# Residual buffer rows of 258 values and a newly searched instruction order in a Performer-attention and Fourier-mixing kernel

## The chip, the cores and the metric

The kernel runs on one core of a Trainium2 chip. The core has five engines with instruction queues of their own: TensorE (PE in the profile, with its weight loads listed apart as PEld), VectorE (DVE), ScalarE (ACT), GpSimd (POOL) and SyncE (SP), which here issues nearly all of the DMA transfers. Each engine takes its instructions strictly in the order in which they stand in the program; between engines, semaphores hold an instruction back until what it needs is there. The metric is the device time of one execution in microseconds (us), lower is better. Everything is computed in fp32.

## What is computed

The reference has two blocks. The first is attention with random positive features for 8 batches of 8 heads, 576 positions and head size 64; the second is a Fourier mixing with a two-layer network behind it.

```python
def phi(x):                                   # 128 features per position
    h = einsum('bhsd,md->bhsm', x, omega) - sum(x * x, -1, keepdims=True) / 2
    return exp(h - max(h, -1, keepdims=True)) / sqrt(m)
q_p, k_p = phi(q * scale), phi(k * scale)
kv, z = einsum('bhsm,bhsd->bhmd', k_p, v), sum(k_p, axis=2)
attn = einsum('bhsm,bhmd->bhsd', q_p, kv) / (einsum('bhsm,bhm->bhs', q_p, z)[..., None] + 1e-6)
x = attn.transpose(0, 2, 1, 3).reshape(8, 576, 512)
u = x + real(fft(fft(x, axis=1), axis=2))
un = (u - mean(u, -1)) / sqrt(var(u, -1) + 1e-6)
out = u + maximum(un @ w_ch1, 0) @ w_ch2      # 512 -> 2048 -> 512
```

The two weight matrices come as 64-bit floats and are turned into fp32 on the chip.

## The kernel before

The work has two parts. **The first part** holds all of the attention, all of the mixing, the conversion of the weights, and the network for the first 512 rows ("plain" blocks, four of 128 rows). **The second part** does the network for the other 4096 rows in eight blocks of 512, by a scheme of seven products in place of eight on halves (`first_of` for the first layer, L1359; `product_of` for the second, L1539).

Attention goes by pairs of heads, 32 pairs, up to three at a time (`attn`). A pair loads its keys and queries (L398, L401) and its values (L406), turns them on TensorE in two groups (`transposed`, L525), evicts these from PSUM on ACT or DVE (L564, L566), multiplies with omega (L644), takes the negative row maximum on DVE (L587) and the exponential on ACT (L604), forms the key-value product (L678, kept by L692 or L694), turns the query features (L525 again), and forms numerator and denominator (L725, L733). DVE then divides (L742, L743, L754) into the tile `x` of the batch.

When the four pairs of a batch are there, `mix` runs its Fourier mixing. Rows are added and subtracted in mirrored pairs ("folds": L782, L784, L788, L798, L811, with small copies at L818, L820 and L823), then TensorE multiplies with cosine and sine tables along the sequence (L844, L854, and L915 for a middle column), the result is evicted (L867) and multiplied along the model size (L894). `residual` brings these products together: ACT copies one half into the first plane of the tile `bmp` (L943), DVE forms difference and sum in the planes `mi` and `pl` (L948, L951), and `summed` adds these to `x` in two instructions, one of them reading backwards (L960, L961). The rows go out to DRAM (L975, L930, L986).

A block of the weights comes as raw 64-bit words (L492) and takes two steps on ACT or POOL (L461; L467 or L469), two on DVE (L472, L474) and one on POOL (L478). When all are converted, `w2_parts` forms the sums of the second weight matrix that the second part needs (L1240, 44 instructions of one size on DVE or POOL) and writes them to DRAM. The plain blocks are normalised (L1072 to L1078), turned (L525, evicted at L1091), multiplied with the first matrix (L1143, rectified at L1127 on DVE or L1129 on ACT) and the second (L1166), and added to their rows (L1179).

What sets the order is not the sequence of the code. Each of these streams is a Python generator that yields a `Step` ahead of its instructions: the engine or a choice of engines, an estimated length, what it waits for, which buffers and PSUM banks it takes and gives back. `Listing.run` picks one waiting step after another and so lays down one order for all engines. For the first part the picks are written out in the string `PICKS`, two characters a step: which of the waiting streams is next, and which engine and bank it gets. There the estimated lengths do not choose anything. For the second part there are no picks, and the planner chooses by estimated times.

A step marked `port=True` is one that the planner does not let run on DVE and POOL at the same time. TensorE runs matmuls in several shapes of its array, which the planner calls modes: the whole array, halves, quarters, and row tiles.

Of the kernel before, what the change touches and what calls it, by code (L numbers as in the profile page):

```python
# [31 lines left out]
NL = 2  # L32
# [7 lines left out]
class Clock(NamedTuple):  # L40
# [25 lines left out]
    "0808d258d8f8c3f8d408d8d6c8c8c8c4e8c8e8d0f8g8f6f858f8g8c8a8b848d2dhd0e2dhd8e8e8b0dhc6d8d488f8ghg8j8c8c890l2k8l6"  # L66
    "i8jhi8j2m8ihlhe888a0l6m4m892j8jhbhl8l818i8i0k888g6k8e2k8i8j878bhd8g8e6i8i4j8i8f8j2j8f8i0k6f8a8b8e8k8i8d2jhehf0"
    "e878i8e8f8i8h8g8g8f4f8g8g8b2d0e8g8b8g898e8h8ghchb6j8b2jhi0j8d6j8h4jhb88hj8j8g0d8e2m8i6m8h8l0m898n8j4h8o8o8g8n8"
    "d2m8m8m8k8k4l8l828l8f8l8a8e2e8f6k8b8f8j8k8e808e878h0j8j4j8d6jhh8j8i0ihehi8ihg4l0l8m8f8g2f6k8k878j0j85878e8h8f8"
    "h8d8h8h888g8b2g8b6g888a078f858i8e8i8f878a2787884h858h878d8d2f8f8g8g8ghc8e4h8i8i8jhb8hhb0j8j6j8j088l8c8j8a8gh78"  # L70
    "88h6h8f852k4k888l8i8j8e0khk6k8k0m2j8j8m8b8i898h8k8a4k8k8j87hh8bhc6j4c8k888g8k8c8d8e872i8f878j888l8b6n858c8n8e8"
    "70m8l8j6o0nhn8n4nhb8j6n2d8lhm0l8l8d8c8gh88k8g4k8k8i8f89868d6h8h888d89868g0g8b8g4h2h8f2h8d8h8hhhhe8f0i8i6j8j468"
    "68g8k8g8g8c2h8h8h088i8g8d6i8i8e8c488i8a878a890hhe8h8d808f8f89868g6h0g858j858l8d8g864j8l8gh88a8k8g8a8b852h8d4i8"
    "70jhi8j8g8c8f6j8k8i8j868c8a8a8j888i870e894i8i2i886ihi4i8f258j868j8b6k8f8j8g8i848a8i8i8d4h8b6i8i8h8i898c8h832ih"
    "e8i2ihi0ih7hi878h8e8i8b6l48hk84hi8j8k898k852k8g0n4nh56k8o8o8k8l883k0o88658p8d8n0p4o8q8k2j898j8o8o8688hn8n8n8kh"
    "k0i8l1n2o6nhj8k8o8n8d2n8n8e878hhgh78k8k84hl8g8j8k8f7e8b458j8j8h8g8e8g8i8h8l8l878b8k2l0k8k88896khc8g8i2i8i0ihg4"
    "i888e8l8c8chd6m8c8b0m8c8l2mhb6m8n8l0m8m6k8h8l8dhehb8n8n8h8g2n8h8o8g4n858e8e8i6l8h8i0l6lhk858k8g882kh98c8j8j868"
    "i86898h8g8a8g84870f8f896g4g8b2h4hhghe868h8j8d6l8l848488898j0jh7854i872i8f8i8i8i8h3k8g6e878k0d4j8g2j8k898i0l2l8"
    "a878dhj8f4l5l8d6l8jhd2k8b5ahj8c8j8i858i8jhg6i8g888j8h8k8e4j8j8c8j8j8b8i882i86878h8h8g4g8a6g8h8a870f8d4h2g8i8i8"
    "ih6838e8j8j8j8d8k83888i896d8j4k868g8m8ahm8f882mhm0m8d4m8m2l0n8lhk8986868h4l2e860b8d8b8e8o8f8n8e8m8m8l8l8l846l8"  # L80
    "h888l84892l8d8l8h8k8l868b878m884m8g8m8l2pho898f8n8fhe0n8n8m8i8c8d8d8b8e8d8j8g8f8n2d0oho4o8g8k8d8k088h8h858b4ih"
    "i2k8j898k8i0k8c8l8l8d4a8e8l898l8983898k8d898dhc88808f8f86880d8g8g868g8e2fhd84864e8d8e8d8d832dha88892d894d8c0dh"
    "c2e4e8d8d2e8f890a8f7g2b8ch88che85878d8d890dhb8b89876b874c0b89hdhd8d8d8c8d882c8c838ch66d7chch7h72c4d0dh78d8d8d8"
    "78d6dh989862b8b8a4c0b8c4b8c6b8e8c89848d8d862dha8d8c3d4e5f2d8che4f6e8e8e7f3e8a8f8f8f8bhd5f488g85898b8a8d8d8d8a8"
    "b8c8d6088898b864ch8hc8chchb0c6d2c8bh2834c8c89896b8bh3852b8b0b898b4b8b6b89268c8c8chc880d4d858883888d8d8dha8d8d8"
    "dhb8483638e758g8g844h8h2i4h840l8l8i8l88858k8k858j8j87h98i8i8b8i88858h862g8b8g8f4f8i67h68j8a87818i8f8e8e8i8a8h8"
    "h8h868g8g8ghc8g8b2h8c8c8c8g8g8g8g878f852h4hhh0h8g8h8e8h838f8c8g878c0g8g4g8f8g8g8e2f8bhehb8e6f4e858d848e868e842"
    "e6f0d8g838c8g8c8547hd8d872fha848e826f4f8c0h2i3f8689hi8i8a8c8g8g8188888c8a89874e0d8b8e898f882g5a8ehg8g8hhb872g8"
    "h8g6chghc0a8i8g1fhhha8h8h8f836h8h858g8a8a08hg4fh42f8ghg4gh78f0d8e8b8f8c698a2fhhhh8h8h8a864e0d892ihd8a8h8e875ah"
    "hhf8c6h2d8h0g8k8i8j8f838i8c4ih48i8h5iha2i8i8ahd8h874g8h8h8h8g8e6g8c828f2h8c8h4hhd8g0gha2g8g4h6i0h8387hi878d888"  # L90
    "g8b278f4h6g8a8h8d8g8g8b8d8e8e890e1f8d808f8i8b2ihh8d8i868i6j4b8h828g8f8h8h4d208ghf8c8c6h2g82858h8e80834g8d8d8e8"
    "a8f888a4b8f6g2e8ehehf8f896b8d8b8b2e4d8b8e6e8ch82d4b6c838d858d8b8d8b818a8d828787278c6c8c4c8b8c808c8c85868c8c864"
    "c848a8a6e298d8ch64d8e8d2e8f8d848d8d87hd8188660e8c8d8d8783862c8d894d8e87h50chd6c868d8d8b838c4ch087870a876b8b2b8"
    "d8a8a8e8e894fhf6f8ah84g6fhche8a8b0f8f438eh62f84868d878c840b8a888b86498a298c8a880bh46b8d864d8d888d870c8c4c8283h"
    "c8687878b0b8b238c846b8b47868808884887h8882b688c8c888c854b8b0b888b894c0c8bhb46858b8b87058a8489h9842484898468818"
    "388848407h4828487268707h68446h4842582h6h70886h787836783478704638a858782286489898688888684476686h2h3058425h5458"
    "265858324858585h246830687878568884224088b868649838183828786692a3589848981h9898686784957h933808282h28284276845h"
    "08988848785h80744h585898a8a82858368091a79ha108325h0h28283h38356408787808181268787878887h7848566878580h58285h4h"
    "3268387818587828688828682818483838381828280h180808"
# [203 lines left out]
def kernel(  # L303
# [149 lines left out]
    def narrow(i, dst, raw):  # L453
# [16 lines left out]
        yield Step(DVE, 0.34, take=("sign",), port=True, bias=0.19)  # L470
# [61 lines left out]
    def transposed(src, name, groups, after, makes, give, order=None):  # L532
# [3 lines left out]
        for j0, j1 in groups:  # L536
            m = j1 - j0
            yield Step(
                PE,
                0.03 + 0.056 * m,  # L540
                mode="rows",
                after=after(j0, j1),
                take=("duo",) + (("turned",) if j0 == 0 else ()),
                give=give(j0, j1), bias=0.14,
            )
# [65 lines left out]
    def attn(n):  # L611
# [18 lines left out]
        def pairs_of(js, *ts):  # L630
# [3 lines left out]
                (0.24 if wide else 0.22) * len(js),  # L634
# [26 lines left out]
        def feature(c):  # L661
# [6 lines left out]
            1.06,  # L668
# [18 lines left out]
        def keep():  # L687
# [23 lines left out]
            1.17,  # L711
# [26 lines left out]
        yield Step(DVE, 0.335, after=(("frame", b),), bias=-0.07)  # L738
# [27 lines left out]
    def mix(b):  # L766
# [8 lines left out]
        def folds(n):  # L775
# [18 lines left out]
            step = Step({DVE: 0.85, POOL: 1.6}, port=True)  # L794
            yield step
            eng = nc.gpsimd if step.eng == POOL else nc.vector
            for dst, o in ((NC3, ALU.add), (1, ALU.subtract)):
# [7 lines left out]
                {DVE: 1.13, POOL: 2.1},  # L805
# [24 lines left out]
        for n, (tab, name) in enumerate(((cs, "cs"), (sn, "sn"))):  # L830
            yield Step(
                PE,
                1.9,
# [42 lines left out]
        for c in range(NC3):  # L876
# [3 lines left out]
                0.97 if c < NL else 0.55,  # L880
# [25 lines left out]
    def middles(b, mid_t, mid_k):  # L906
        yield Step(PE, 0.5, mode="halves", after=(("fold", b, 0), "cs"), take=("bank",))
# [19 lines left out]
    def mirrored(b, x):  # L927
        yield Step(SP, 1.15, 2.6, after=(("sum", b, 1), ("sum", b, 2)), makes=("uh", b), kb=512, bias=-0.92)
# [6 lines left out]
    def residual(b, c, x, abb, mid_k):  # L935
# [4 lines left out]
        bmp = fft.tile([P, 3, KD], F32, name="bmp", tag="bmp", bufs=2)  # L940
        bs, mi, pl = (bmp[0:np_, n, :] for n in range(3))
# [13 lines left out]
        def summed(g, left, right):  # L955
            step = Step({DVE: 0.68, POOL: 1.3}, port=True)
# [102 lines left out]
    def norm_of(j, t, i, pool, dst, block=None, after=()):  # L1059
# [11 lines left out]
        yield Step(DVE, 1.12 if pool is mlpp else 1.01, after=after, bias=4.0 if after else -0.23)  # L1071
# [10 lines left out]
        yield Step(PE, 0.25, mode="rows", take=("duo",), give=("u",))  # L1082
# [598 lines left out]
```

## Time and profile before

| | |
|---|---|
| median of 3 runs | 1186.29 us (1183.14 to 1188.23) |
| profiled execution, its own time | 1184.3 us |
| its span, first to last instruction | 1182.5 us |
| granted TensorE clock, mean | 0.996 |
| busy in the span: PE, PEld | 1140.8 us, 1016.3 us |
| busy in the span: DVE, ACT, POOL | 767.1 us, 435.1 us, 412.4 us |
| HBM read, written | 179.24 MB, 43.25 MB |

The profile is of one execution. The kernel's lines carry the numbers that the text uses (L960 is line 960). In groups of instructions, "x16" is the number of instructions, then comes their busy time in us, the mean of one in ns, and behind the bar how long the engine had stood idle just before them and what ended that wait. A matmul of fp32 stands in the trace as two records. "Busy" for TensorE counts from the start of a matmul to its modelled end, and neighbours overlap, so the pace is read from start to start. An idle time with the releaser "issue" is one in which the engine waited for nothing that the profile shows.

### The profile page before, as it was taken

The numbers are of one execution on the slowest core, as the hardware profiler recorded it, in microseconds if no ns is written. First come the engines' busy times: TensorE is split into PE (matmuls) and PEld (weight loads), VectorE is DVE, ScalarE is ACT, GpSimd is POOL, SyncE is SP. The second block draws the span as 40 slices with busy tenths as digits, with TensorE's granted clock in tenths as the row PEclk, the third lists the DMA queues.
The fourth block names the chain that finished last, engine by engine and source line by source line (L and its number), as shares of the span: only waits on it lengthen the run. The fifth ranks groups of instructions, "written<-read, shape, count | busy, mean of one in ns | idle before, by whom it ended". The sixth has DMA issues, their size and how long they took to land.

```text
span 1182.5 us, 32511 instructions
## 1 busy us (share of the span) xinstructions
PE 1140.8 (96%) x13045; PEld 1016.3 (86%) x13045; DVE 767.1 (65%) x1591; ACT 435.1 (37%) x1423; POOL 412.4 (35%) x483
## 2 busy tenths in 40 slices
PE   8988889999999999999999999999999999999998
PEld 7767775968777968998998998899999899899898
DVE  6999797798788764754664564563574474475255
ACT  7887776545667312112112112212212212211211
POOL 2455443233224116225225314413513412522421
PEclk9999999999999999999999999999999999999999
DMA  7777657565644154783683593594496397388155
GB/s 233 205 213 230 214 169 218 171 217 178 204 118 132 42 162 137 241 272 102 197 295 104 161 312 108 142 313 152 105 308 197 86 280 238 80 244 266 44 166 200
DMA packets 167222, 220.43 MB, mean 186 GB/s; under 512 B 50080, under 2 KB 81056, under 8 KB 167072
## 3 DMA queue, kind: packets, MB, share of 16 engines
q1 hardware_dynamic: 166576, 218.09, 59.9%
q8 instruction: 103, 1.69, 0.6%
q14 instruction: 47, 0.39, 0.1%
q10 hardware_dynamic: 496, 0.26, 0.1%
HBM read 179.24 MB, written 43.25 MB: 188 GB/s over the span
## 4 chain that ended last, share of the span: by engine, by line
PE 83%; DVE 7%; DMA 4%; ACT 3%; issue 2%; SPq 0%; POOL 0%; DVEq 0%; ACTq 0%; POOLq 0%
PE banks L1359 33%; PE banks L1539 28%; PE banks L1166 4%; PE banks L644 4%; PE banks L1143 4%; PE banks L525 3%; DMA wl<-w2l 3%; PE banks L678 2%; ACT e L604 2%; PE banks L725 2%; DVE nmx L587 1%; PE banks L894 1%; PE banks L844 1%; DMA kq<-in_q_dram 1%; DVE w L474 1%
## 5 line engine op out<-in xcount | busy, mean ns | idle before, releaser
L1539 PE MATMUL banks<-wl,sums 128*128 128x128 f32 x1792 | 217.6, 275 | 0.0
L1539 PEld LDWEIGHTS banks<-wl,sums 128*128 128x128 f32 x1792 | 208.6, 192 | 0.0
L1345 DVE CUSTOM_DVE_ANT_0 hid<-banks,s 128x256 f32<-128x256 f32 x192 | 81.1, 424 | 190.9 <-PE banks L1359 190.4
L604 ACT ACTIVATE e<-banks,nmx 128x128 f32<-128x128 f32 x576 | 157.8, 406 | 41.8 <-DVE nmx L587 41.5
L1373 ACT ACTIVATE s<-banks 128x256 f32<-128x256 f32 x192 | 73.5, 383 | 254.5 <-PE banks L1359 243.6
L1359 PE MATMUL banks<-unT,w 128*128 128x256 f32 x704 | 166.4, 379 | 0.0
L1359 PEld LDWEIGHTS banks<-unT,w 128*128 128x128 f32 x704 | 133.4, 190 | 18.1 <-issue 0.5
L1514 ACT ACTIVATE s<-banks 128x128 f32<-128x128 f32 x168 | 46.6, 277 | 261.1 <-PE banks L1539 224.2
L1579 POOL TENSOR_TENSOR ur<-ur,part 128x512 f32<-128x512 f32 x32 | 47.1, 1472 | 269.7 <-ACT part L1572 195.4
L1359 PE MATMUL banks<-tt,w1s 128*128 128x256 f32 x512 | 126.2, 379 | 0.0
L1359 PEld LDWEIGHTS banks<-tt,w1s 128*128 128x128 f32 x512 | 97.2, 190 | 13.3
L1539 PE MATMUL banks<-wl,hid 128*128 128x128 f32 x768 | 99.6, 276 | 7.1 <-DMA wl<-w2l 7.0
L1519 DVE TENSOR_TENSOR part<-banks,s 128x128 f32<-128x128 f32 x168 | 48.9, 291 | 86.5 <-PE banks L1539 85.4
L1539 PEld LDWEIGHTS banks<-wl,hid 128*128 128x128 f32 x768 | 94.1, 192 | 9.4 <-DMA wl<-w2l 8.2
L587 DVE TENSOR_REDUCE nmx<-banks 128x8 f32<-128x1024 f32 (+1 forms) x96 | 89.2, 951 | 15.3 <-PE banks L644 12.7
L644 PE MATMUL banks<-om,kqT 64*64 64x128 f32 (+1 forms) x2088 | 82.9, 278 | 10.6 <-DVE kqT L564 2.8
L644 PEld LDWEIGHTS banks<-om,kqT 64*64 64x64 f32 (+1 forms) x2088 | 67.1, 141 | 23.3 <-ACT e L604 4.1
L1359 PE MATMUL banks<-unT,w1s 128*128 128x256 f32 x320 | 79.5, 379 | 0.0
L1539 PE MATMUL banks<-wl,hs 128*128 128x128 f32 x576 | 75.0, 275 | 0.4 <-DVE part L1519 0.4
L1539 PEld LDWEIGHTS banks<-wl,hs 128*128 128x128 f32 x576 | 70.1, 192 | 0.9 <-DVE part L1519 0.6
L1426 POOL TENSOR_TENSOR hs<-hid,hs 128x256 f32<-128x256 f32 x64 | 50.0, 782 | 57.6 <-issue 37.5
L1359 PEld LDWEIGHTS banks<-unT,w1s 128*128 128x128 f32 x320 | 60.4, 190 | 8.6
(133 smaller groups left out, 1843.4 us busy)
## 6 DMA issues: line engine op xcount, KB each, us to landing
wl<-w2l SPq DMA_DIRECT2D x392, 256.0 KB
raw<-in_moe_w_ch_dram SPq DMA_DIRECT2D x32, 512.0 KB
kq<-in_k_dram SPq DMA_DIRECT2D x32, 288.0 KB
kq<-in_q_dram SPq DMA_DIRECT2D x32, 288.0 KB
vd<-in_v_dram SPq DMA_DIRECT2D x32, 288.0 KB
u<-us SPq DMA_DIRECT2D x36, 256.0 KB
ur<-us SPq DMA_DIRECT2D x36, 256.0 KB
out_dram<-ur SPq DMA_DIRECT2D x34, 256.0 KB
```

Of the source, the lines that this page charges most:

```text
L587: nc.vector.tensor_reduce(nmx[:, :, 0:num], pps[:, :, 0 : MF * num].rearrange("p b (c m) -> p b c m", m=MF), axis=AX.X, op=ALU.max, negate ...
L604: nc.scalar.activation(out=e[:, c + (i if num == 1 else 0), :], in_=pps[:, i, MF * c : MF * c + MF], func=AF.Exp, bias=nmx[:, i, c : c + 1],)
L644: nc.tensor.matmul(pps[cols, c, MF * m : MF * m + MF], lhsT=kqT[rows, j, cols], rhs=om2[rows, :],)
L1143: nc.tensor.matmul(hp[:, 0:TP], lhsT=w1[:, dc, 128 * fc : 128 * fc + 128], rhs=unTs[key][:, dc, :], start=(dc == 0), stop=(dc == NDC - 1),)
L1166: nc.tensor.matmul(yp[:, 0:DM], lhsT=hs[fc][:, 128 * i : 128 * i + 128], rhs=w2[:, fc, :], start=(fc == 0), stop=(fc == NFC - 1),)
L1345: nc.vector._custom_dve(TENSOR_ADD_SAT, out=o, in0=ps, in1=sb, s0=FMAX, s1=0.0)
L1359: nc.tensor.matmul(ps[:, 0:HT].rearrange("f (b q) -> f b q", q=Q), lhsT=left(dc), rhs=right(dc), start=start and dc == 0, stop=(dc == D2 - 1),
L1373: nc.scalar.activation(out=s[:], in_=ps[:, 0:HT], func=AF.Copy)
L1426: nc.gpsimd.tensor_tensor(out=o, in0=l, in1=r, op=op)
L1519: nc.vector.tensor_tensor(out=part[:, t, 128 * m : 128 * m + 128], in0=ps[:, 0:128], in1=saved[with_][:], op=ALU.add,)
L1539: nc.tensor.matmul(ps[:, 0:128], lhsT=left[:, f], rhs=wls[j, i, n][:, f], start=start and f == 0, stop=(f == 3), skip_group_check=True,)
L1579: eng.tensor_tensor(out=o, in0=o, in1=other, op=ALU.add)
```

## The change

Three things are changed: the length of a row of `bmp`, estimated lengths of fifteen steps, and the string `PICKS`.

```diff
-        bmp = fft.tile([P, 3, KD], F32, name="bmp", tag="bmp", bufs=2)
-        bs, mi, pl = (bmp[0:np_, n, :] for n in range(3))
+        bmp = fft.tile([P, 3, KD + 1], F32, name="bmp", tag="bmp", bufs=2)
+        bs, mi, pl = (bmp[0:np_, n, 0:KD] for n in range(3))
...
-            step = Step({DVE: 0.68, POOL: 1.3}, port=True)
+            step = Step({DVE: 0.67, POOL: 1.24}, port=True)
...
-        yield Step(DVE, 0.34, take=("sign",), port=True, bias=0.19)
+        yield Step(DVE, 0.44, take=("sign",), port=True, bias=0.19)
...
-                (0.24 if wide else 0.22) * len(js),
+                (0.25 if wide else 0.23) * len(js) + (0.07 if wide and len(js) == 1 else 0.0),
...
-            step = Step({DVE: 0.85, POOL: 1.6}, port=True)
+            step = Step({DVE: 0.88, POOL: 1.68}, port=True)
...
-                {DVE: 1.13, POOL: 2.1},
+                {DVE: 1.13 if n else 1.35, POOL: 2.2 if n else 2.5},
...
-        yield Step(PE, 0.5, mode="halves", after=(("fold", b, 0), "cs"), take=("bank",))
+        yield Step(PE, 0.69, mode="halves", after=(("fold", b, 0), "cs"), take=("bank",))
...
 PICKS = (
-    "0808d258d8f8c3f8d408d8d6c8c8c8c4e8c8e8d0f8g8f6f858f8g8c8a8b848d2dhd0e2dhd8e8e8b0dhc6d8d488f8ghg8j8c8c890l2k8l6"
+    "4818f8d0f808e3e8d848d4d8d6e20838b8c4f6e8g8a8f8a8f8f8b4ehb8e8e8d4e0dhd8b2d8f8a838e478a8a6bhdh92d8e888b4dhc8b6d8"
...
```

KD is 257, so the three planes of `bmp` now begin at the values 0, 258 and 516 of a partition instead of 0, 257 and 514; the tile has two buffers. The other changed lengths are of the same kind: transposes (0.03 + 0.056 m to 0.055 + 0.0505 m), key-value product (1.06 to 1.09), numerator (1.17 to 1.21), the products with the tables (1.9 to 1.94; 0.97 and 0.55 to 0.9 and 0.51), the division (0.335 to 0.42), the storing of the mirrored rows (1.15 to 1.3), the statistics (1.12 or 1.01 to 1.01) and the turning of normalised rows (0.25 to 0.3).

The picks are all new: each engine gets another order in the first part. The instructions are the same ones in number, but for the choices that a step leaves open: which engine does it, and whether an eviction or a product is taken by one engine or the other. The table has the instructions of the first part whose engine shares differ, counted in the two programs.

| | before | after |
|---|---|---|
| L1240, sums of the second matrix, DVE / POOL | 30 / 14 | 21 / 23 |
| L811, fold, DVE / POOL | 20 / 12 | 14 / 18 |
| L798, fold, DVE / POOL | 20 / 12 | 16 / 16 |
| L820 and L823, small copies, DVE / POOL | 18 / 6 | 9 / 15 |
| L960 (and L961 alike), residual sum, DVE / POOL | 16 / 24 | 18 / 22 |
| L1127 / L1129, rectifying, DVE / ACT | 33 / 31 | 28 / 36 |
| L564 / L566, evicting 512 columns of kqT, DVE / ACT | 9 / 23 | 12 / 20 |
| L564 / L566, evicting 640 columns of kqT, DVE / ACT | 11 / 21 | 8 / 24 |
| L467 / L469, first scaling of the weights, POOL / ACT | 12 / 20 | 14 / 18 |

In the second part every engine has the same instructions in the same order as before.

More of the change, by code (lines that the diff above doesn't have):

```diff
@@ L737, in attn @@
                 )
-        yield Step(DVE, 0.335, after=(("frame", b),), bias=-0.07)
+        yield Step(DVE, 0.42, after=(("frame", b),), bias=-0.07)
         x = xts[b % 2]
@@ L879, in mix @@
                 PE,
-                0.97 if c < NL else 0.55,
+                0.9 if c < NL else 0.51,
                 mode="whole" if c < NL else "halves",
@@ L927, in mirrored @@
     def mirrored(b, x):
-        yield Step(SP, 1.15, 2.6, after=(("sum", b, 1), ("sum", b, 2)), makes=("uh", b), kb=512, bias=-0.92)
+        yield Step(SP, 1.3, 2.6, after=(("sum", b, 1), ("sum", b, 2)), makes=("uh", b), kb=512, bias=-0.92)
         for s in range(2):
@@ L1070, in norm_of @@
         rstd = small.tile([P, 1], F32, name="rstd", tag="rstd")
-        yield Step(DVE, 1.12 if pool is mlpp else 1.01, after=after, bias=4.0 if after else -0.23)
+        yield Step(DVE, 1.01, after=after, bias=4.0 if after else -0.23)
         nc.vector.bn_stats(out=st[:], in_=u[:])
@@ L1081, in norm_of @@
             return
-        yield Step(PE, 0.25, mode="rows", take=("duo",), give=("u",))
+        yield Step(PE, 0.3, mode="rows", take=("duo",), give=("u",))
         b, tp = got()
```

74 lines of the change are left out of this document (37 added, 37 removed).

## The prediction

> **What bounds the kernel now.** I read the page's busy shares by slice first, then busy time by stretch, then the chain of waits, the engines' groups in the first part, and last the timeline round single waits.
>
> ```profile
> PE   8988889999999999999999999999999999999998
> DVE  6999797798788764754664564563574474475255
> ACT  7887776545667312112112112212212212211211
> POOL 2455443233224116225225314413513412522421
> PEclk9999999999999999999999999999999999999999
> ```
>
> TensorE (PE) is full nearly everywhere at an unthrottled clock. Only the first seven or so slices (29.6 us each) have room, and there VectorE (DVE) is almost as full. The chain shows where the second part begins:
>
> ```profile
> 421.49 10.50 PE banks L1166 x24
> 431.99 41.44 PE banks L1359 x192
> ```
>
> The last product of the plain blocks (L1166) runs straight into the first of the seven-product blocks (L1359), so the first part ends at 432.0 with nothing waited for. I cut it at the place where TensorE stops having holes, the end of the 16th pair of heads (its last product, L733, ends at 202.3):
>
> ```profile
> 200.96 1.15 PE L725 MATMUL banks<-kv,qeT 128*64 128x65 f32 x32
> 201.94 0.40 PE L733 MATMUL banks<-kv,qeT 128*64 128x65 f32 x8
> core 0: us, PE busy (x) PEld busy (x) DVE busy (x) ACT busy (x) POOL busy (x), PEclk, DMA share, GB/s
> 0.00:202.30 202.30, 176.56 (x4027) 147.12 (x4027) 173.30 (x353) 156.26 (x503) 89.71 (x95) 0.98 0.71 216
> 202.30:432.00 229.70, 225.24 (x4095) 178.25 (x4094) 178.52 (x415) 124.30 (x443) 66.68 (x73) 1.00 0.47 144
> 432.00:1182.50 750.50, 738.97 (x4928) 690.88 (x4927) 415.31 (x823) 154.58 (x479) 256.03 (x316) 1.00 0.62 191
> ```
>
> Up to there TensorE is without work for 202.3 - 176.6 = 25.7 us, while DVE works 173.3 and ScalarE (ACT) 156.3 of 202.3. From there to 432.0 it lacks 229.7 - 225.2 = 4.5. All that an order of the first part can win from idle time is therefore about 30 us, and 26 of them lie ahead of the 16th pair. One of these holes is no fault of the order; TensorE stopped in the middle of a group with nothing to wait for:
>
> ```profile
> 138.34 0.97 PE L678 MATMUL banks<-vd,e 64*64 64x65 f32 x49 [3.82 <-issue]
> ```
>
> **The change part by part.** *The second part*, 750.5 us, has the same instructions in the same order on all five engines in the changed program; it counts 0.
>
> *The rows of 258.* The buffer's second plane begins at value 258 instead of 257, the third at 516 instead of 514; reads and writes stay as long as they were.
>
> ```profile
> L951 DVE TENSOR_TENSOR bmp<-banks,bmp x48: 283/292/298, 58.7 to 425.1; 128x128 f32<-128x128 f32 x32, 64x128 f32<-64x128 f32 x16
> L960 DVE TENSOR_TENSOR x<-x,bmp x16: 366/420/1522, 102.0 to 425.3; 128x257 f32<-128x257 f32 x11, 64x257 f32<-64x257 f32 x5
> ```
>
> Half of the L951 writes go to the plane that begins at an odd value, half to the one that begins at an even value, and all 48 lie between 283 and 298 ns; a price of odd starts would split them. L960 has a single 366 against a median of 420, so the bound is a gain of 16 x 0.054 = 0.9 us of DVE time over the whole part, and no reason for a loss. I take 0.
>
> *The changed step lengths* are numbers for the planner; with the order written out they decide nothing on the chip. 0.
>
> *The new order* is all that is left. The total work is the same but for its split: over the first part DVE gives up 9 of its 30 subtractions at L1240, 6 of 20 adds at L811, 4 of 20 at L798 and the 9 small copies at L820 and L823 to GpSimd (POOL), and 5 of 33 rectifications at L1127 to ACT. What matters is what is done by the end of the 16th pair, counted in both orders.
>
> DVE up to the 16th pair's division (L743): the new order has 5 evictions of 640 columns less (ACT takes them), 3 of L1240 less, 1 of L782 less, 2 of L692 less and 3 small copies less, and as more 2 of L798, 2 of L564 with 64 columns, 2 with 256, one of L1179, two residual sums (each an L960 and an L961, one of 128 and one of 64 rows) and a small copy.
>
> ```profile
> L564 DVE COPY qeT<-banks 128x256 f32<-128x256 f32 x20 | 7.4, 417 | 0.4 <-PE banks L525 0.2
> L564 DVE COPY kqT<-banks 128x640 f32<-128x640 f32 x7 | 5.7, 813 | 0.0
> L782 DVE TENSOR_TENSOR half<-x 128x1024 f32<-128x1024 f32 x4 | 4.9, 1219 | 0.1
> L961 DVE TENSOR_TENSOR x<-x,bmp 128x255 f32<-128x255 f32 x3 | 4.6, 1518 | 0.0
> L798 DVE TENSOR_TENSOR half<-half 128x257 f32<-128x257 f32 x8 | 4.4, 546 | 0.1
> L564 DVE COPY qeT<-banks 128x64 f32<-128x64 f32 x18 | 3.1, 215 | 4.6 <-PE banks L525 4.6
> L692 DVE COPY kv<-banks 128x130 f32<-128x130 f32 x10 | 2.9, 290 | 1.3 <-PE banks L678 1.2
> L1240 DVE TENSOR_TENSOR sums<-w,sums 128x512 f32<-128x512 f32 x2 | 1.4, 687 | 0.0
> L823 DVE COPY mid<-half 64x1 f32<-64x1 f32 x4 | 0.6, 144 | 0.0
> ```
>
> Less: 5 x 0.813 + 3 x 0.687 + 1.219 + 2 x 0.290 + 3 x 0.144 = 8.4. More: 2 x 0.546 + 2 x 0.215 + 2 x 0.417 + 0.69 (L1179, at the L1240 duration) + 0.14 + the two sums, 4 x 0.42 = 1.7 if unhindered = 4.9. DVE has 3.5 us less; with the 128-row sum held up as in the L961 row (1.518 for 0.42) 2.4.
>
> TensorE up to the same point: one key-value product less (36 at L678, 72 records), 18 transposes more, 8 plain products of L1143 (16 records) and 4 of L1166 (8 records) more.
>
> ```profile
> 298.81 2.05 PE L1143 MATMUL banks<-unT,w 128*128 128x128 f32 x16
> 300.80 1.15 PE L725 MATMUL banks<-kv,qeT 128*64 128x65 f32 x32
> 305.97 1.28 PE L678 MATMUL banks<-vd,e 64*64 64x65 f32 x72
> 307.18 0.78 PE L525 MATMUL banks<-ident,e 64*128 64x64 f32 x18
> 307.88 2.19 PE L644 MATMUL banks<-om,kqT 64*64 64x128 f32 x72
> 396.21 9.20 PE L1143 MATMUL banks<-unT,w 128*128 128x128 f32 x80
> 405.24 1.33 PE L844 MATMUL banks<-cs_sb,fold 128*128 128x160 f32 x8
> ```
>
> From start to start: 80 records of L1143 take 9.03, so 16 take 1.8; L1166 takes 10.50 / 24 = 0.44 each, so 8 take 3.5; 18 transposes 0.70; the key-value group 1.21. Sum +1.8 + 3.5 + 0.7 - 1.2 = +4.8 us of work put into the stretch that has 25.7 us of holes, and so taken out of the 229.7 us that have none.
>
> *Changes of array shape.* Neighbouring matmuls of the first part change between whole array, halves, quarters and row tiles 248 times now and 217 times in the new order; behind the 16th pair 132 and 117. The price: the 16-record L1143 group above takes 1.99 to the next group's start against 1.8 at the steady pace, 0.18 for going in and out together, 0.09 each; bounds 0 and 0.18. Ahead of the 16th pair the holes cover it; behind, 15 x 0.09 = 1.4 us less (0 to 2.7).
>
> *What is unpriced:* how long DVE and TensorE wait for each other in the new order ahead of the 16th pair. Counted with each group's mean, ACT has some 8 us more to do and POOL some 6 us more, in what DVE waits for by then. ACT has room (156 of 202); POOL's room is not free:
>
> ```profile
> 188.84 2.87 POOL L478 TENSOR_TENSOR w<-w,raw 128x512 uint32<-128x512 uint32 x2 [3.27 <-ACT raw L461]
> 189.03 1.52 DVE L960 TENSOR_TENSOR x<-x,bmp 128x257 f32<-128x257 f32 x1
> 190.47 1.52 DVE L961 TENSOR_TENSOR x<-x,bmp 128x255 f32<-128x255 f32 x1
> ```
>
> Two DVE sums that read two buffers stretch from 0.42 to 1.52 while POOL adds, and the second ends just behind POOL's second add. This L960 (1.1), the three of L961 (3.3) and the eight of L798 (0.6, against the 472 of the whole part) lose 5.0 us to 89.7 us of POOL, 0.06 a microsecond, so 6 us more POOL cost about 0.4. Of DVE's 3.5 I count half, since DVE idles 29.0 of these 202.3 us anyway: -1.7 + 0.4. Loads move too: the four loads of a pair and the weights' raw blocks stand in another order on SP's queue. Each is still issued as many buffers ahead as before, and that hides it; the price I take is 0, and without that cover another hole like the 3.82 above.
>
> The sum: TensorE's work brought forward -4.8, DVE -1.3, shapes -1.4: -7.5. With waits all better (DVE's 3.5 whole, shapes 2.7, the 3.82 hole gone) -4.8 - 3.5 - 2.7 - 3.8 = -14.8; with nothing of the early work reaching the end, -1.4. The profiled execution took 1184.3 (span 1182.5 and 1.8 around it); -7.5 gives 1176.8. The median of the runs, 1186.3, lies 2.0 above it: 1178.8, a gain of 0.6%.
>
> **The rivals.** *The order gains only the shapes.* The 16th pair ends 4.8 us later than I have it because DVE and ACT, not the place of TensorE's work, pace the front. For it: ACT's 8 us more by then. Against: TensorE work moved forward needs no DVE at that moment. 1186.3 - 1.4 = 1184.9.
>
> *POOL takes the fold's place on the path (slower).* In the new order 3 more steps of L811 and 2 more of L798 lie on POOL, and the fifth to seventh mixing have all of both there.
>
> ```profile
> L811 POOL TENSOR_TENSOR fold<-half 128x384 f32<-128x384 f32 x12 | 11.8, 1002 | 5.0 <-DVE half L798 4.7
> L811 DVE TENSOR_TENSOR fold<-half 128x384 f32<-128x384 f32 x20 | 10.3, 555 | 0.7 <-POOL half L798 0.5
> L798 POOL TENSOR_TENSOR half<-half 128x257 f32<-128x257 f32 x12 | 9.4, 783 | 15.7 <-DVE half L788 15.2
> L844 PE MATMUL banks<-cs_sb,fold 128*128 128x160 f32 x64 | 10.8, 312 | 0.0
> L1240 POOL TENSOR_TENSOR sums<-big,sums 128x512 f32<-128x512 f32 x4 | 5.7, 1432 | 16.9 <-DVE sums L1240 13.1 <-issue 3.8
> ```
>
> A step of two adds takes 2 x (1.002 - 0.555) = 0.9 or 2 x (0.783 - 0.472) = 0.6 longer there: 3.9 us in all on the way to L844. The moved work fills POOL with 9 x 1.43 + 6 x 1.0 + 4 x 0.78 = 22 us more. If each of these 19 instructions also holds one DVE add back by half its own length, DVE loses 11 us; a third of it at times when TensorE has nothing else gives 3.7. Together 1186.3 + 7.6 = 1193.9. It decides where TensorE's holes behind the 16th pair exceed today's 4.5 us by more than the gain of 6 to 7. Against: L844 never waited (0.0), and the plain products fill in.
>
> [...]
>
> *All waits better:* 1186.3 - 14.8 = 1171.5.
>
> **How the numbers follow.** My forecast has a chance of 0.42, the shapes alone 0.30, POOL on the path 0.17, all waits better 0.11. Half a per cent, about what a measurement can tell from no change, is 5.9 us here: faster means below 1180.4, slower above 1192.2. The forecast, with an own range of 1174 to 1183, lies below the line with 0.33 of its 0.42; with the last rival 0.44 faster. Same: 0.09 + 0.30 + 0.03 of the POOL case = 0.42. Slower: 0.14. The range reaches to most of the outer cases: 1170 to 1191.
>
> **What would show it.** The second part again 750.5 us. The first matmul of L1359 at 424 to 426 instead of 432; the 16th pair ended at about 201, with DVE near 171 busy and TensorE near 181. Behind it some 223 us with at most 5 us of holes. L951 at 292 ns and L960 at 420 as before. I am wrong if the 16th pair ends behind 206, if TensorE waits for L811 or L798 by more than 2 us, or if a load or a hole without releaser costs more than the 3.8 us of now.

## The result and the profile after

| | before | after |
|---|---|---|
| median, runs on the same chip | 1187.26 us (4 runs, 1183.14 to 1188.87) | 1177.96 us (4 runs, 1177.42 to 1178.66) |
| profiled execution, its own time | 1184.3 us | 1177.47 us |
| its span | 1182.5 us | 1175.7 us |

The ratio of the times is 0.9927, with a 95% interval of 0.9900 to 0.9954: the changed kernel is faster by 0.7%. The forecast was 1178.8. In one experiment below, the moved products put back, two of twelve executions were more than 1.5% slower than the fastest, and its median, range and ratio leave them out.

First the busy times on the page of after.

```profile
PE 1139.7 (97%) x13045; PEld 1019.1 (87%) x13045; DVE 745.3 (63%) x1562; ACT 433.8 (37%) x1426; POOL 441.3 (38%) x509
```

The number of matmul records is the same, 13045. DVE went from 767.1 to 745.3, POOL from 412.4 to 441.3, and TensorE's busy time hardly moved. So the gain must lie in when TensorE works, not in how much. Next the timeline of after round the two places where the prediction cut the span, the end of the 16th pair's L733 and the first L1359, and busy time by the stretches between them.

```profile
201.13 0.40 PE L733 MATMUL banks<-kv,qeT 128*64 128x65 f32 x8
...
419.82 5.31 PE L1166 MATMUL banks<-w,ht 128*128 128x512 f32 x12
424.97 1.03 PE L1359 MATMUL banks<-unT,w 128*128 128x256 f32 x4
```

```profile
0.00:201.60 201.60, 179.46 (x4004) 151.20 (x4005) 165.58 (x351) 161.69 (x518) 97.83 (x96) 0.97 0.70 209
201.60:425.00 223.40, 218.36 (x4121) 175.30 (x4118) 164.62 (x388) 117.56 (x429) 87.62 (x97) 0.99 0.52 159
425.00:1175.70 750.70, 741.91 (x4929) 692.55 (x4927) 415.14 (x823) 154.60 (x479) 255.84 (x316) 1.00 0.61 190
```

Ahead of the 16th pair's end the time fell from 202.3 to 201.6, behind it from 229.7 to 223.4, and the second part took 750.7 after 750.5. Of 6.8 us of span, 6.3 come from the middle stretch. There TensorE's busy time fell from 225.24 to 218.36, while it lacks 223.4 - 218.4 = 5.0 us of work now and lacked 4.5 before. The stretch became shorter because work had left it, not because holes in it closed. This holds beyond one execution: the stretch took 222.8 us in the profiles of the new order alone and of after run again, and 228.7 in that of the rows alone, which keep the old order (all three among the experiments below). The stretch ahead scatters more than it changed here: five profiles of the new order, two of them with products added only further back, ended the 16th pair at 194.9 to 204.2 us, and the two of the old order at 202.3 and 204.3.

What TensorE waited for in the first 425 us of after, the longest sums (in all, times, longest):

```profile
PE banks L678 <- issue: 5.9, 4, 2.5
PE banks L644 <- issue: 3.5, 2, 2.3
PE banks L678 <- ACT e L604: 3.1, 4, 1.7
PE banks L525 <- issue: 1.8, 2, 1.4
...
PE banks L725 <- issue: 1.4, 1, 1.4
```

No row of this view names L811 or L798. The largest sums carry "issue": TensorE stopped though nothing that the profile shows held it back, 5.9 + 3.5 + 1.8 + 1.4 = 12.6 us in all. In before these rows sum to 6.0.

### The profile page after: what moved, and what is told of

Read it like the earlier page. It is cut to its first block, busy times and chain, and to the rows that moved or that the text cites. A ratio compares the mean times of both kernels' runs of the same rounds, so it can differ in the third digit from the quotient of the medians.

```text
span 1175.7 us, 32543 instructions
## 1 busy us (share of the span) xinstructions
PE 1139.7 (97%) x13045; PEld 1019.1 (87%) x13045; DVE 745.3 (63%) x1562; ACT 433.8 (37%) x1426; POOL 441.3 (38%) x509
## 4 chain that ended last, share of the span: by engine, by line
PE 84%; DVE 5%; ACT 4%; DMA 3%; issue 2%; SPq 1%; POOL 0%; DVEq 0%; POOLq 0%; ACTq 0%
PE banks L1359 33%; PE banks L1539 27%; PE banks L1143 5%; PE banks L644 4%; PE banks L1166 4%; DMA wl<-w2l 3%; PE banks L525 3%; ACT e L604 3%; PE banks L678 2%; PE banks L725 2%; DVE nmx L587 1%; PE banks L844 1%; PE banks L894 1%; PE banks L854 1%; DVE w L474 1%
## 5 line engine op out<-in xcount | busy, mean ns | idle before, releaser
L1359 PE MATMUL banks<-unT,w 128*128 128x256 f32 x704 | 166.3, 379 | 0.0
L1359 PEld LDWEIGHTS banks<-unT,w 128*128 128x128 f32 x704 | 133.2, 190 | 18.3 <-issue 0.5
L1579 POOL TENSOR_TENSOR ur<-ur,part 128x512 f32<-128x512 f32 x32 | 46.9, 1465 | 270.0 <-ACT part L1572 195.7
L1359 PE MATMUL banks<-tt,w1s 128*128 128x256 f32 x512 | 126.2, 379 | 0.0
L1359 PEld LDWEIGHTS banks<-tt,w1s 128*128 128x128 f32 x512 | 97.1, 190 | 13.5
L644 PE MATMUL banks<-om,kqT 64*64 64x128 f32 (+1 forms) x2088 | 83.1, 283 | 8.0 <-issue 3.5
L644 PEld LDWEIGHTS banks<-om,kqT 64*64 64x64 f32 (+1 forms) x2088 | 69.1, 145 | 18.4 <-issue 5.6
L1359 PE MATMUL banks<-unT,w1s 128*128 128x256 f32 x320 | 79.5, 379 | 0.0
L478 POOL TENSOR_TENSOR w<-w,raw 128x512 uint32<-128x512 uint32 x32 | 43.6, 1370 | 69.7 <-ACT raw L461 30.0
```

The lines of the kernel that those rows point to most:

```text
L644: nc.tensor.matmul(pps[cols, c, MF * m : MF * m + MF], lhsT=kqT[rows, j, cols], rhs=om2[rows, :],)
L1359: nc.tensor.matmul(ps[:, 0:HT].rearrange("f (b q) -> f b q", q=Q), lhsT=left(dc), rhs=right(dc), start=start and dc == 0, stop=(dc == D2 - 1),
L1579: eng.tensor_tensor(out=o, in0=o, in1=other, op=ALU.add)
```

## The experiments

All ratios are to the kernel before, run beside each on the same chip.

**The three parts of the change apart.** First the rows of 258 in the kernel before:

```diff
-        bmp = fft.tile([P, 3, KD], F32, name="bmp", tag="bmp", bufs=2)
+        bmp = fft.tile([P, 3, KD + 1], F32, name="bmp", tag="bmp", bufs=2)
```

> The kernel of before with the rows of 258 alone. My theory (the order is everything): no change, 1186 to 1188 us, ratio 0.998 to 1.002. Rival (the even starts speed up the residual's instructions on DVE and POOL): 3 us or more of the 8 to 9 us gained, ratio 0.997 or less. In the trace of the changed kernel the GpSimd sums that read the third plane took 730 ns instead of 637; if the row length does that and not the order, it shows here too.

Measured: 1186.48 us (12 runs), ratio 0.9984 (0.9964 to 1.0004). A change can't be told from none; the interval leaves room for a gain of up to 4 us. Second, the kernel after with that line put back to rows of 257, so that the new order stands alone:

```diff
-        bmp = fft.tile([P, 3, KD + 1], F32, name="bmp", tag="bmp", bufs=2)
+        bmp = fft.tile([P, 3, KD], F32, name="bmp", tag="bmp", bufs=2)
```

> The new order with rows of 257. My theory: the whole gain, 1177 to 1180 us, ratio 0.991 to 0.995. Rival: at least 3 us of the gain are lost, 1181 us or more.

Measured: 1177.87 us, ratio 0.9897 (0.9864 to 0.9930). The order alone has all of the gain that the whole change had (0.9927). The changed step lengths are in this kernel too; alone they leave the first part's order as it is, and they weren't run by themselves.

**Places and engines apart.** A pick has two characters, the stream and the choice of engine. One kernel has the new places with the engine choices of before, the other the reverse; 187 steps differ. One line of the new picks and what became of it in the first kernel, then one of the old picks and what became of it in the second:

```diff
-    "b4e890ehe2e898h8ghb8j808a4i8i87880i878h488j8ahi8i8g8b8c8h0h88876h2g8i8f0h8e8h8e8g8g8c6fha8e4fh88c0i6i8j8g8i8g8"
+    "b4eh90e8e2e898h8ghb8j808a4i8i87880i878h488j8ahi8i8ghb8c8h0h88876h2g8i8f0hhe8h8e8g8g8c6f8a8e4f888c0i6i8j8g8i8g8"
...
-    "i8jhi8j2m8ihlhe888a0l6m4m892j8jhbhl8l818i8i0k888g6k8e2k8i8j878bhd8g8e6i8i4j8i8f8j2j8f8i0k6f8a8b8e8k8i8d2jhehf0"
+    "i8jhi8j2m8ihl8e888a0l6m4mh92j8j8bhl8l818ihi0k888g6khe2k8i8j878bhd8g8e6i8i4j8i8f8j2j8f8i0k6f8a8b8e8k8i8d2j8e8f0"
```

> The new order of steps, but each step that has a choice runs on the engine that it had before (187 steps differ: evictions, folds, sums of the second weight matrix, residual sums). If the places of TensorE's work and its changes of shape make most of the gain, as I summed it (6.2 of 7.5), it stays at 1179 to 1182 us. If unloading DVE onto POOL and ACT makes it, it goes back to 1185 us or more.

> The old order of steps with the engines that the new order chooses. If the places make the gain: 1184 to 1189 us. If the engines make it: 1181 us or less.

Measured: 1236.60 us, ratio 1.0402 (1.0373 to 1.0431), and 1240.85 us, ratio 1.0432 (1.0403 to 1.0462). Every time that an expectation named was missed by some 50 us; 1236.60 lies within the "1185 us or more" of the rival, but not for its reason. Waits of TensorE in the first 480 us of the new places with the old engines:

```profile
PE banks L1143 <- DVE ht L1127: 4.8, 3, 3.7
PE banks L678 <- ACT e L604: 4.3, 2, 2.7
PE banks L525 <- DVE x L754: 3.9, 5, 1.4
PE banks L525 <- DVE kv L692: 3.9, 3, 2.9
```

No single wait stands out; there are many small ones, on DVE and ACT in turn, and TensorE is without work for 65 us of the first part, where after has 27. The clock adds to it: 54.6 us of the first part ran at half the clock, worth up to 27 us (half of them, an estimate), where before has 6.8 us of that kind (last section). My reading is that each step stands where it does because an engine is free at that moment; the runs show only that neither half of the order is good without the other. The two halves have no shares of their own that could be added up, so whether the gain is owed to places or to engines has no answer here.

**What a microsecond of TensorE is worth on each side of the 16th pair, and what a change of array shape costs.** Into the kernel after go 64 small products whose results are not read: in the last plain block four behind each of its 16 hidden products, or one behind each of their 64 matmuls (the same work, 128 changes of shape in place of 32), or four behind each hidden product of the first plain block, which lies ahead.

```diff
+                if j == 3 and dc == NDC - 1:
+                    for _ in range(4):
+                        nc.tensor.matmul(
+                            hp[0:64, 256:384], lhsT=ident[0:64, 0:64], rhs=ident[0:64, :], start=False,
+                            stop=True, skip_group_check=True
+                        )
```

In the second form the condition is `j == 3` alone and the range 1, in the third `j == 0`.

> The changed kernel with 64 idle matmuls of 64x64 by 128 columns (their result is not read) in the last plain block, behind the 16th pair, four behind each of its 16 hidden products: 32 more changes of shape. TensorE has no holes there, so their whole length shows: 64 x 0.11 = 7 us and 32 changes at 0.09 = 2.9 us, 1186 to 1190 us. Rival (the end is not set by TensorE there): less than 3 us, below 1181 us.

> The same 64 idle matmuls in the same block, but one behind each single matmul: 128 more changes of shape instead of 32. By my price of 0.09 us a change it is 8.6 us slower than the grouped one. At a price of nothing: the same time. At the upper bound of 0.18: 17 us slower.

> The same 64 idle matmuls, grouped by four, in the first plain block, which lies ahead of the 16th pair. My theory (the holes of TensorE ahead of the 16th pair take work without cost, which is why the plain products brought forward were worth their length): less than half of what the grouped ones cost behind, at most 1183 us. Rival (TensorE's own sequence paces the front too, and work put there costs what it costs anywhere): the same as behind, 1186 us or more.

Measured: 1198.09 us, ratio 1.0108 (1.0065 to 1.0151); 1214.50 us, ratio 1.0264 (1.0229 to 1.0299); 1187.03 us, ratio 0.9994 (0.9967 to 1.0020). The price of a change can be read from the timelines of the first two (start, length, records; L1152 is the added product). Grouped:

```profile
388.98 1.16 PE L1143 MATMUL banks<-unT,w 128*128 128x128 f32 x8
390.06 1.08 PE L1152 MATMUL banks<-ident 64*64 64x128 f32 x8
391.08 1.16 PE L1143 MATMUL banks<-unT,w 128*128 128x128 f32 x8
```

Spread:

```profile
392.07 0.49 PE L1143 MATMUL banks<-unT,w 128*128 128x128 f32 x2
392.49 0.43 PE L1152 MATMUL banks<-ident 64*64 64x128 f32 x2
392.85 0.49 PE L1143 MATMUL banks<-unT,w 128*128 128x128 f32 x2
```

Grouped, eight records of each take 391.08 - 388.98 = 2.10 us with two changes. Spread, the same sixteen take 4 x (392.85 - 392.07) = 3.12 with eight. A change costs 1.02 / 6 = 0.17 us. The stretch behind the 16th pair agrees: 264.7 us spread, 240.5 grouped. Of the 24.2 us between them some 7 belong to the clock, which was granted at half for 17.1 us of the spread one (steps took 1.7 times as long there, such as 351 ns for 205), and the other 17 make 0.18 for each of 96 changes. The medians differ by 16.4, but the granted clock was lower in all six spread runs (0.983 to 0.988, grouped 0.986 to 0.995), so they are no second check. The spread form came near the 17 us of the upper bound in its expectation. The grouped one missed its 1186 to 1190, because each product is two records: eight take 1.02 us, so all 128 take 16, not 7.

By the ratios to before, the 64 grouped products cost (1.0108 - 0.9927) x 1187 = 21 us behind and (0.9994 - 0.9927) x 1187 = 8 us ahead. That looks as if a microsecond ahead were worth less than half of one behind, but the profiles do not bear it out: both spans were 1187.5 us. Behind, TensorE's busy time rose by 17.6 and the stretch by 17.1 us; ahead, busy time rose by 16.6 and the stretch by 15.8, to 217.4, so hardly anything was absorbed. The runs ahead scatter from 1178.56 to 1191.02, and their median missed my "at most 1183" and met the rival's "1186 us or more". What is shown is that work put ahead is not free merely because of where it lies. My reading is that it must fall into a hole, and that this work, in front of the first block's rectification, takes the place of no wait.

**The moved products put back.** The kernel after, with four products of L1166 and eight of L1143 (and what hangs on them) moved from just ahead of the turning of the 16th pair's query features to just behind the pair. In the picks, a piece of two lines:

```diff
-    "80h298i8i8d8i888a8f8c8d0d8c8f8g8d8f8f8d6f2f8d8c8e8g87858e8a8f86808dhd8dhdha8a8c5e2e846f0g2eh88g8b8c8ch98c82834"
-    "c8c8c896c8c852c8c0d4c8d6d8cha0ch88c8c8b298d4dhd6dhb868a0b8c8b2c8d848chc8b4c856e7dhe0dhdh82e688a8e878dhd8d8dh80"
+    "80h298i8i8d8i888a8f8c8d0d8c8f8g8d8f8f8d6f2f8d8f8g87858e8b8f86808dhd8dhdh46e0f2dh98f8c8chb8c82830c8c8c896c8c862"
+    "c858c858b5d7c8c8a0d4c8d6d8ch80ch68c8c8b278d4dhd6dhb878a0b8c8b2c8d848chc8b4c866e7dhe0dhdh82e688a8e878dhd8d8dh80"
```

> The changed kernel with the two last products of the first plain block's second layer and the two first products of the second block's first layer (4.8 us of TensorE time by my prediction) taken from ahead of the 16th pair and put some 2 us behind it. My theory (plain work ahead of the 16th pair goes into holes, so each microsecond of it is a gain): the 16th pair ends as before and the rest takes 4.8 us more, 1181 to 1184 us. Rival (work put ahead costs its length there too, so its place between the two stretches does not matter): the 16th pair ends about 4 us earlier and the total stays, 1177 to 1180 us. The idle matmuls put ahead cost about half of what they cost behind, which lies between the two: then 1179 to 1181 us.

The kernel after was run again beside it, on the same chip:

> The changed kernel itself once more, so that the others of this group can be set beside it on one chip: 1177 to 1179 us, ratio 0.990 to 0.995.

Measured: 1184.43 us (ten runs, 1176.66 to 1189.60), ratio 0.9968 (0.9944 to 0.9992), and for after 1175.68 us, ratio 0.9910 (0.9876 to 0.9945). That lies just above the 1181 to 1184 of my theory and clear of the rival's 1177 to 1180. The timeline of TensorE at that place shows the reason. After:

```profile
190.88 2.31 PE L644 MATMUL banks<-om,kqT 64*64 64x128 f32 x72
193.12 3.70 PE L1166 MATMUL banks<-w,ht 128*128 128x512 f32 x8
196.66 1.05 PE L1143 MATMUL banks<-unT,w 128*128 128x128 f32 x8
197.90 1.16 PE L1143 MATMUL banks<-unT,w 128*128 128x128 f32 x8 [0.19 <-ACT e L604]
199.19 1.03 PE L525 MATMUL banks<-ident,e 64*128 64x64 f32 x18
```

With the products moved behind:

```profile
189.95 2.29 PE L644 MATMUL banks<-om,kqT 64*64 64x128 f32 x72
198.27 1.48 PE L525 MATMUL banks<-ident,e 64*128 64x64 f32 x18 [6.03 <-ACT e L604]
200.07 2.00 PE L725 MATMUL banks<-kv,qeT 128*64 128x65 f32 x32 [0.32 <-ACT qeT L566]
```

Between the product with omega and the turning of the features TensorE has to wait for ACT's exponentials in any case. In after, the plain products fill those 6 us; without them the same time is a hole, and the 16th pair ends at 202.5, not earlier than the 201.5 of after. The stretch behind grew to 226.8 against 223.4 and 222.8 in the two profiles of after, so by 3.4 to 4.0. The rest of the 8.7 us between the medians (6.9 by the ratios) is not explained as sharply. Some 2 us lie in the clock, which was granted at half from inside the hole on. From the turning to the pair's end, 4.23 us pass where after needs 2.34, so at the full clock the pair would have ended near 200.6. That is 0.9 earlier than in after, and 0.9 is what this execution was ahead by at the product with omega already; 5.3 us of work less gained nothing more. The window with the half clock:

```profile
196.10:202.90 6.80, 4.31 (x70) 4.04 (x72) 1.35 (x6) 3.04 (x12) 0.98 (x1) 0.50 1.00 325
```

And the second part took 757.5 us in this profile, 750.7 for the same instructions in after; the ten times scatter over 13 us.

**Fewer instructions for TensorE.** The holes without a releaser fit the loading of TensorE's instructions (last section). If so, fewer matmuls in the dense places should close some. The product with omega can run in row tiles of full width, half as many matmuls for the same rows, and `NWIDE` says for how many pairs it does:

```diff
-    NWIDE = 6
+    NWIDE = 16
```

Three kernels have it: the one after with 16, the one before with 16, and the one after with 24.

> The changed kernel with the feature products of pairs 6 to 15 in row tiles of 64x128 as in pairs 0 to 5: 180 matmuls less ahead of the 16th pair, at some 0.18 us more TensorE time a pair. In the profile of the changed kernel TensorE stands still eight times in the middle of a group with no releaser, 13 us in all, each time until shortly after a 16 KB instruction load. If those holes come from TensorE running out of instructions, fewer matmuls make them fewer: 1172 to 1177 us, with less than 10 us of such holes. If not: 1178 to 1181 us by the 1.8 us of longer products.

> The kernel of before with row tiles of 64x128 for the feature products of pairs 6 to 15 too. With the new order this took 14 us off, and the holes without releaser went from eight to three. If it works by sparing TensorE instructions in a stretch where it runs out of them, the old order, whose holes of that kind are five with 6.1 us, gains less than the new one, 3 to 8 us: 1179 to 1184 us. If it works by shorter TensorE work or fewer changes of shape alone, both orders gain alike: 1172 to 1176 us. If the gain belongs to the new order alone: 1186 us or more.

> The changed kernel with the wide row tiles for pairs 0 to 23. Behind the 16th pair TensorE has no holes but the two without releaser (2.1 us above their normal pace), and the wide form costs 0.02 us more a product, 8 pairs x 9 x 0.02 = 1.4 us: within 2 us of the kernel with 16 wide pairs. If the gain came from fewer changes of shape or shorter products, it would go on: 5 us or more below it.

Measured: 1164.20 us, ratio 0.9823 (0.9795 to 0.9852); 1182.92 us, ratio 0.9953 (0.9935 to 0.9971); 1170.84 us, ratio 0.9853 (0.9831 to 0.9875). With 16 wide pairs the kernel beats both others. Its first two stretches, and what TensorE waited for in its first 416 us:

```profile
0.00:194.10 194.10, 175.97 (x3641) 150.41 (x3643) 166.29 (x351) 160.72 (x518) 97.37 (x96) 0.98 0.72 218
194.10:415.80 221.70, 217.34 (x4124) 174.01 (x4121) 165.29 (x388) 117.66 (x429) 87.54 (x97) 1.00 0.52 159
```

```profile
PE banks L678 <- issue: 3.5, 4, 1.6
PE banks L678 <- ACT e L604: 2.8, 4, 1.3
PE banks L725 <- issue: 2.1, 1, 2.1
```

360 records fewer, the stretch ahead 7.5 us shorter, and the holes without releaser down from 12.6 to 5.6 us in these sums. Of the 7.5 us, 4.0 are idle time of TensorE (22.1 to 18.1), which the holes account for, and 3.5 are busy time. In the busy time three things are mixed. The products became a little cheaper: in after 2088 records of L644 are busy for 64.9 + 18.2 = 83.1 us, here 1728 for 42.6 + 38.2 = 80.8. By the records' shapes the first part has 11 changes fewer, some 1.9 us at 0.17. And one stretch at half the clock is missing ahead, worth up to 1.7 us (half of its 3.4, an estimate). The clock was better throughout: all six runs were granted 0.993 to 0.997, the ten of after 0.988 to 0.995, so some 5 us of the whole gain can be the clock's (an estimate from some 0.004 of 1177 us), whether or not fewer holes are the reason for it.

The first of the three came out below its 1172 to 1177, with the holes below 10 us as the theory had it. The old order gained within the 3 to 8 us expected, but its profile does not show the mechanism: the stretch ahead took 202.9 us, 202.3 in before, and the holes went from 6.0 to 4.4. (Two of before's holes are longer than 0.7 us, not the five that the expectation has.) With 24 the gain doesn't grow, as it should if shorter products carried it. (For the changes of shape this is no test: there are 208 after 210.) But it is smaller than with 16, by 3.6 us by the ratios, where within 2 were expected. Why, no run settles.

## Why the prediction came true, and where it was off

*The order is the whole change.* Held within the noise: rows alone 0.9984, order alone 0.9897.

*TensorE's work brought forward, -4.8.* Held, in size and mechanism. The stretch behind is 6.3 us shorter where the forecast had 4.8 + 1.4 = 6.2, and putting the moved products back shows the hole that they fill. What it rests on was put too broadly, though: a stretch ahead that covers added work because it has holes would have made the added products of the first plain block free, and they cost 8 us by the medians and more in the profile. My reading is that a hole covers what can run in it at that moment, as the one of 6.03 us does for the moved products.

*DVE, -1.3.* The result ahead, -0.7, is near it, but by a different sum, and by luck: with ends from 194.9 to 204.2 us for the same instructions, one profile can't tell 0.7 from 1.3. DVE's busy time to the 16th pair fell by 7.7 us, not by 2.4 to 3.5, although the instructions are those that were counted. Its groups ahead of the 16th pair's end, after:

```profile
L798 DVE TENSOR_TENSOR half<-half 128x257 f32<-128x257 f32 x10 | 4.2, 424 | 0.2
L1240 DVE TENSOR_TENSOR sums<-w,sums 128x512 f32<-128x512 f32 x1 | 0.7, 674 | 0.0
```

and two of before from the same view:

```profile
L798 DVE TENSOR_TENSOR half<-half 128x257 f32<-128x257 f32 x8 | 4.4, 546 | 0.1
L1240 DVE TENSOR_TENSOR sums<-w 128x512 f32<-128x512 f32 x2 | 2.1, 1033 | 0.0
```

Ten instructions of L798 now take less than eight did, and the L1240 pair that went away had taken 1033 ns each, not 687. The term for DVE's additions beside POOL's work had the wrong sign: POOL works 8.1 us more here (97.83 after 89.71; the forecast had some 6), yet these additions were held up less. In before one of the eight of L798 took 1405 ns and one of L1240 1382 ns, each while POOL was at work on an L478 (at 50.56 for 1.44 us, at 195.45 for 1.28); the other seven of L798 took 418 to 428 ns. In after all ten took 418 to 429, and none of them met POOL. My reading is that the order decides how often two such instructions meet, so POOL's total could not give the price. What TensorE did ahead adds up to the -0.7: it was busy for 2.9 us more, its waits for other engines fell from some 19 to some 11 us, and its holes without releaser rose from 5.7 to 10.0. It idles 22.1 us there, of which the forecast had 20.

*The clock, no term.* The prediction called the clock unthrottled. But before had two stretches of 3.4 us at half the clock ahead of the 16th pair, and after has three there and one behind; each costs up to 1.7 us by an estimate (last section). Part of the scatter of the ends comes from these: after ended the pair at 201.5 with 10.2 us at half, after run again at 204.2 with 17.1, and the new order alone at 197.8 with 3.4. With half of that time taken off, the three lie at 195.7 to 196.4, the rows alone at 197.5 and before at 198.9. The two kernels with products added behind come to 191.5 and 192.8; why they are lower still, no run shows.

*Changes of shape, 15 x 0.09 = -1.4.* The price was too low: 0.17 us each, measured between the whole array and a quarter, so 2.5, within the bounds of 0 to 2.7. (By the array shapes of the records the traces have 134 changes and 121, 13 fewer for the 15, and 2.2.) With it the sum behind is -7.0 to -7.3, and 0.5 us more of holes there make it -6.5 to -6.8, where -6.3 was measured. The prediction read its price from the first start of a group to the first start of the next, so the step into the group was left out; in the grouped form a step from one shape to the other takes 0.20 us, after 0.11 within a group, and the first step behind it is slower too.

*The rows of 258, 0.* Held for the time, but "L951 at 292 ns and L960 at 420 as before" held only for DVE's L960. The tile `bmp` in after:

```profile
L951 DVE TENSOR_TENSOR bmp<-banks,bmp x48: 271/279/292, 62.2 to 418.5; 128x128 f32<-128x128 f32 x32, 64x128 f32<-64x128 f32 x16
...
L960 POOL TENSOR_TENSOR x<-x,bmp x22: 628/691/2545, 63.1 to 414.8; 128x257 f32<-128x257 f32 x19, 64x257 f32<-64x257 f32 x3
L961 POOL TENSOR_TENSOR x<-x,bmp x22: 625/728/1174, 63.7 to 415.9; 128x255 f32<-128x255 f32 x19, 64x255 f32<-64x255 f32 x3
L960 DVE TENSOR_TENSOR x<-x,bmp x18: 407/419/1515, 76.3 to 418.7; 128x257 f32<-128x257 f32 x13, 64x257 f32<-64x257 f32 x5
```

L951 became 13 ns cheaper at the median, and POOL's sums dearer, 637 to 691 and 634 to 728. The rows of 258 did this, not the order. With the rows alone:

```profile
L951 DVE TENSOR_TENSOR bmp<-banks,bmp x48: 270/281/288, 60.4 to 425.4; 128x128 f32<-128x128 f32 x32, 64x128 f32<-64x128 f32 x16
...
L961 POOL TENSOR_TENSOR x<-x,bmp x24: 630/722/900, 61.4 to 426.6; 128x255 f32<-128x255 f32 x21, 64x255 f32<-64x255 f32 x3
```

With the new order alone the two stand at 293 and 638 ns, as in before (292 and 634). The argument that a price of odd starts would split the 48 writes of L951 was wrong: the writes go to the two planes in turn, and those of the plane that had begun at an even value became cheaper by as much as the others.

*The second part the same.* 750.7 after 750.5, closer than it had to be: the same instructions took 746.0 to 757.5 us in the other profiles. A small fact in the prediction was not exact: on SP's queue two loads of L1065 stand one place further among the weight loads. Nothing in the time answers to it.

*Loads and holes.* The prediction called itself wrong if a hole without releaser cost more than 3.8 us. No single one did, the longest is 2.5 us. But they sum to 12.6 us where before had 6.0, and 8 of them are longer than 0.7 us where before had 2. The price of 0 for them was too low, and the forecast came true in spite of it: fewer waits for the other engines and more of these holes partly cancel ahead of the 16th pair.

*POOL on the path.* TensorE has no wait for L811 or L798, and none ahead of L844's matmuls; that rival fell.

## What to carry to other kernels

Cut the span where the bounding engine stops having holes, and price a reordering by the work that it takes out of the full stretch and puts into the holes of the other; here that gave the size (6.2 forecast, 6.3 measured), while the count of the other engines' work gave little. Look at more than one profile before you judge a term of a microsecond or two. An order and its choices of engine are one thing: half of a good order cost 4% (1.0402 and 1.0432). Where matmuls are short and dense, count them too: fewer of them went with fewer holes here (360 records fewer, and 5.6 us of holes after 12.6).

## What the hardware showed that was not expected

**TensorE seems to stop for its own instructions.** Two of the holes without releaser in after, on the timeline:

```profile
40.98 1.03 PE L678 MATMUL banks<-vd,e 64*64 64x65 f32 x53
44.49 0.56 PE L678 MATMUL banks<-vd,e 64*64 64x65 f32 x19 [2.48 <-issue]
...
134.66 2.18 PE L644 MATMUL banks<-om,kqT 64*64 64x128 f32 x67
139.17 0.66 PE L644 MATMUL banks<-om,kqT 64*64 64x128 f32 x5 [2.34 <-issue]
```

The group of 72 products stops in its middle. The DMA queues in the window 41.5 to 43.2, with packets, MB and share, then the same queue on the page:

```profile
q1 hardware_dynamic: 144, 0.44, 103.5%
q8 instruction: 1, 0.02, 4.8%
```

```profile
q8 instruction: 103, 1.69, 0.6%
```

103 loads of 16 KB come to one for each 2 x 13045 / 103 = 253 records of matmuls and weight loads; with 16 wide pairs there are 100 loads for 2 x 12685 records, 254 for each. In the trace the load of this window starts at 41.76 and takes 1.29 us; TensorE goes on 1.44 us after it has landed. At all eight holes without releaser of more than 0.7 us in the first part, such a load landed 1.27 to 1.49 us before TensorE went on; together these holes are 12.2 us of idle time. Before has two such holes, 3.8 and 0.8 us long. With 16 wide pairs there are three, 5.1 us in all. The other 56 of the 64 loads in the first part of after have no such hole behind them. Seven of the eight fell into moments when the data queue (q1, 103.5% in this window) took more than three quarters of the DMA engines' time; but so did some fifteen others that left no hole, so what sets these eight apart stays open. That these loads cause the holes is inferred from their timing and from the runs with fewer instructions; no run moved a load alone.

**The clock at half for 3.4 us.** Right behind the hole that ends at 139.17:

```profile
139.30:142.70 3.40, 3.40 (x59) 3.07 (x60) 1.57 (x3) 2.37 (x11) 0.99 (x1) 0.50 0.90 279
```

The granted clock is 0.50 for 3.40 us. The first part of after has four such stretches, before has two, and the kernel with new places and old engines twelve, most of them 3.4 and some 6.8 us long. In after each of the four starts 0 to 1.2 us behind the end of a hole without releaser of 0.96 us or more, and not every such hole has one. In the 3.40 us just ahead of the four TensorE was busy for only 1.06 to 1.96 us, and ahead of the two in before for 1.33 and 1.78; but in the 3.40 us up to 44.5 in after it was busy for 0.92, and the clock stayed at 1.00 in the next 3.40. What brings such a stretch on is therefore not shown. Within the stretch above, the 32 records of L725 that start at 139.76 take 2.00 us, where 32 take 1.15 at the full clock (at 200.15), 1.7 times as long; at a clock of 0.50 a stretch of 3.40 us loses at most half of itself, the 1.7 us used above, an estimate. The profiled execution of the new order alone had a single such stretch and took 1168.65 us, where its five other runs took 1177.33 to 1180.06.
